# Strassen's method for the second layer's second product in two of three passes, on one Trainium2 core

## The chip, the cores and the metric

The kernel runs on one core of one Trainium2 chip. The metric is the device time of one execution in microseconds (us). Before the change the median of three runs was 808.29 us (807.82 to 812.54). Smaller is better.

## The reference, cut to what matters

An attention of Nyström type over four batches gives `x` of 2304 tokens by 512. Two layers without bias follow, each of two products:

```python
def _moe_ref(x, w_in, w_out):            # first layer, w_in 512 x 2048, w_out 2048 x 512
    h = x @ w_in
    sp = np.where(h > 20.0, h, np.log1p(np.exp(np.minimum(h, 20.0))))
    return ((h * np.tanh(sp)) @ w_out).astype(np.float32)

def _moe2_ref(x, w_in, w_out):           # second layer, the same shapes
    h = x @ w_in
    r = np.maximum(h, 0.0)
    g = r * r
    return (g @ w_out).astype(np.float32)
```

The change concerns the last line, `g @ w_out` of the second layer: 2304 x 2048 times 2048 x 512.

## The kernel before, in words

Both layers compute in float32 split in two: each operand is a high part (rounded to the matmul's fp32r type) and a low part (the rest), and a product is three matmuls, high by high, high by low and low by high. A matmul here loads 128x128 of one operand as weights and streams up to 512 columns of the other.

The second layer runs in three passes (index 0, 1, 2; called pass one, two and three below), each over 768 tokens as two blocks of 384. A pass goes over eight quads `Q{pass}{j}`, each 256 of the 2048 hidden columns. The first product of a quad already uses a form of Strassen's method with seven products (`Quad.p`, L995 to L1013): step `p(k)` is six matmuls of 384 columns into one PSUM room of the kind `y` (there are two, and a few of the first go elsewhere). ScalarE copies the first product (`s`, L1015), and VectorE makes the rest by seven additions `d(k)` of 128x384 (L1030), each of one product in PSUM to one sum in SBUF; a `d` frees the room that a later `p` needs. Then `r` squares the positive part (L1038, VectorE, 128x768, twice a quad), `h` makes the high part (L1043, ScalarE) and `g` the low part (L1048, VectorE).

The second product of a quad is `y(k)` for six blocks of 128 tokens (L1050 to L1063): the token block of `g` is the weight, and `w_out` streams, six matmuls of 512 columns each:

```python
for i in range(2):
    gh, gl, oh, ol = self.gh[:, i, ts], self.gl[:, i, ts], self.w[7 + 2 * i], self.w[8 + 2 * i]
    nc.tensor.matmul(ps, gh, oh, start=(j == 0 and i == 0), stop=False)
    nc.tensor.matmul(ps, gh, ol, start=False, stop=False)
    nc.tensor.matmul(ps, gl, oh, start=False, stop=(j == NQ - 1 and i == 1))
```

Over the eight quads the sums stay in PSUM, in three rooms of two banks (two of the kind `h`, one `at`). At the end of a pass `e(k)` (L1065) copies them to SBUF, and `o(k)` (L1072) sends them out.

The weights of the second layer are decoded from the inputs by `Unit` (steps `d, lo, st, ab, cl, ad, hi, lw`, L284 to L356), during the first layer and pass one. `hi` and `lw` make the high part on ScalarE and the low part on GpSimd; `sv` writes them to DRAM, and each quad of each pass loads seven tiles for the first product (`a`) and four for the second (`b`), 256 KB each, from there. `Forms` (`X{pass}`) makes the combinations of the inputs for the first product, with the low parts on GpSimd (`l`, L973).

The order of all steps of all engines is written out by hand in the string `PROGRAM`; no scheduler moves anything. Each engine runs its steps strictly in that order, and so does the one DMA queue, SyncE's.

Of the kernel before, what the change touches and what calls it, by code (L numbers as in the profile page):

```python
# [19 lines left out]
P = 128  # L20
TT = 384
# [13 lines left out]
NPASS = 3  # L35
MORE = 12
# [22 lines left out]
    d.cv U8.st f.tq@at B1.r0 c.ET B1.n1@y c.pv@y t0.c0 f.Tq e.sk B1.z1 B1.r1 U6.hi U5.cl U8.ab B1.n2@y e.tq@h B1.z2
    c.cr B1.r2 f.sq t0.c1 c.cv B1.n3@y+4 e.Tq d.mi U5.ad e.Sk B1.r3 U5.hi B1.z3 t0.g0 B1.n4@y+3 B1.r4 e.tl@y U6.lw  # L60
# [135 lines left out]
def nystrom_mish_relu2(  # L196
# [81 lines left out]
    class Unit:  # L278
# [876 lines left out]
```

## Time and profile before

| What | us |
|---|---|
| median of 3 runs | 808.29 (807.82 to 812.54) |
| the profiled execution, its own time | 807.35 |
| its span, first to last instruction | 805.5 |
| the first layer and the attention, up to the first product of pass one | 418.95 |
| pass one of the second layer | about 418.95 to 550 |
| passes two and three, to the last matmul | about 550 to 801 |

The times in the rows are microseconds from the start of the span. PE is TensorE's matmuls, PEld its weight loads, DVE is VectorE, ACT ScalarE, POOL GpSimd, SP SyncE. Matmuls are pipelined: one that is listed with 0.33 us starts its successor sooner, so what a matmul costs in a stream is the distance from one start to the next.

### The profile page before, as it was taken

The page shows a single profiled execution, that of the slowest core. Times are in us where ns is not written, and L with a number is a line of the kernel's source. Part 1 is how long each engine was busy: PE and PEld are TensorE (multiplying, and loading weights), DVE is VectorE, ACT ScalarE, POOL GpSimd, SP SyncE. Part 2 cuts the span into 40 slices and gives each one's busy share as a digit, 9 for nine tenths or more (in the row PEclk, how much of TensorE's full clock was granted, in tenths as well). Part 3 has the DMA queues.
Part 4 walks back from the last instruction along what each step waited for, and adds up shares of the span by engine and source line. Part 5 has one row for each costly group of instructions (what it writes and reads, how often), then busy time and mean ns, then how long its engine had stood idle before and what let it go on. Part 6 is the DMA issues. An engine that isn't in the chain of part 4 may idle for free.

```text
span 805.5 us, 14157 instructions
## 1 busy us (share of the span) xinstructions
PE 778.9 (97%) x5502; PEld 701.8 (87%) x5502; DVE 544.3 (68%) x898; ACT 338.3 (42%) x543; POOL 224.5 (28%) x172
## 2 busy tenths in 40 slices
PE   5798999999999999999998999999999999999997
PEld 4567988889999899999997899898889889798985
DVE  7989776756547967886978787767444454444552
ACT  5686898745443643647533423411122111211101
POOL 1345343231323643424462352531112000000000
PEclk9999999999999999999999999999999999999999
DMA  9972543222031455476568877879656666666603
GB/s 288 302 177 54 144 143 103 81 61 72 27 105 53 143 185 180 159 251 229 175 213 280 292 249 274 281 261 350 206 168 213 202 202 195 207 213 195 196 28 79
DMA packets 74435, 145.64 MB, mean 181 GB/s; under 512 B 8576, under 2 KB 21888, under 8 KB 74368
## 3 DMA queue, kind: packets, MB, share of 16 engines
q1 hardware_dynamic: 74368, 144.74, 56.3%
q8 instruction: 43, 0.70, 0.4%
q14 instruction: 24, 0.20, 0.1%
HBM read 116.92 MB, written 27.79 MB: 180 GB/s over the span
## 4 chain that ended last, share of the span: by engine, by line
PE 87%; DVE 6%; ACT 2%; DMA 2%; issue 1%; POOL 0%; DVEq 0%; ACTq 0%; POOLq 0%
PE y L793 8%; PE O L1061 8%; PE O L1060 8%; PE y L795 8%; PE y L794 8%; PE O L1059 8%; PE P L1007 7%; PE P L1008 7%; PE P L1009 7%; PE h L793 4%; PE h L795 4%; PE h L794 4%; PE m L778 2%; DMA rawwo<-in_moe_w_out_dram 1%; DVE lmq L434 1%
## 5 line engine op out<-in xcount | busy, mean ns | idle before, releaser
L1030 DVE TENSOR_TENSOR C<-U,P 128x384 f32<-128x384 f32 x96 | 51.8, 550 | 51.2 <-PE P L1009 50.0
L1043 ACT CAST gh<-C 128x768 fp32r<-128x768 f32 x48 | 39.3, 835 | 103.3 <-DVE C L1038 103.1
L1030 DVE TENSOR_TENSOR U<-U,P 128x384 f32<-128x384 f32 x72 | 39.8, 552 | 59.4 <-PE P L1009 58.4
L793 PE MATMUL h<-ah,mh 128*128 128x384 f32 (+1 forms) x256 | 79.1, 309 | 0.0
L795 PE MATMUL h<-ah,ml 128*128 128x384 f32 (+1 forms) x256 | 78.0, 305 | 0.0
L794 PE MATMUL h<-al,mh 128*128 128x384 f32 (+1 forms) x256 | 77.9, 304 | 0.0
L1048 DVE TENSOR_TENSOR gl<-C,gh 128x768 fp32r<-128x768 f32 x48 | 49.5, 1036 | 27.8 <-ACT gh L1043 27.4
L345 POOL TENSOR_TENSOR rawwo<-rawwo 128x512 int32<-128x512 int32 x32 | 37.0, 1158 | 109.7 <-DVE rawwo L329 68.5
L866 DVE TENSOR_TENSOR gl<-s,gh 128x768 fp32r<-128x768 f32 x48 | 53.6, 1117 | 20.1 <-ACT gh L856 20.0
L907 DVE TENSOR_TENSOR acc<-acc,y 128x384 f32<-128x384 f32 x72 | 39.1, 548 | 39.3 <-PE y L795 39.0
L1017 ACT COPY U<-P 128x384 f32<-128x384 f32 x24 | 11.5, 478 | 105.3 <-PE P L1009 105.3
L793 PEld LDWEIGHTS h<-ah,mh 128*128 128x128 f32 x256 | 48.5, 190 | 6.2 <-issue 2.7
L845 ACT ACTIVATE s<-h 128x768 f32<-128x768 f32 x48 | 38.8, 813 | 26.0 <-PE h L795 22.4
L795 PEld LDWEIGHTS h<-ah,ml 128*128 128x128 f32 x256 | 48.6, 190 | 0.0
L794 PEld LDWEIGHTS h<-al,mh 128*128 128x128 f32 x256 | 48.6, 190 | 0.0
L856 ACT CAST gh<-s 128x768 fp32r<-128x768 f32 x48 | 39.8, 834 | 15.8 <-PE y L795 15.4
L1038 DVE SCALAR_TENSOR_TENSOR C<-C 128x768 f32<-128x768 f32 x48 | 44.9, 958 | 0.8
L312 ACT ACTIVATE rawwo<-rawwo 128x512 f32<-128x512 uint32 x32 | 21.7, 678 | 30.2 <-DMA rawwo<-in_moe_w_out_dram 24.4
L342 POOL TENSOR_TENSOR wa<-rawwi 128x512 int32<-128x512 int32 x16 | 20.1, 1261 | 46.9 <-DVE rawwi L329 45.9
L315 DVE SCALAR_TENSOR_TENSOR rawwo<-rawwo 128x512 uint32<-128x512 uint32 x32 | 24.9, 778 | 10.5 <-ACT rawwo L312 10.3
L312 ACT ACTIVATE rawwi<-rawwi 128x512 f32<-128x512 uint32 x32 | 21.8, 684 | 21.3 <-DMA rawwi<-in_moe_w_in_dram 21.3
L335 POOL TENSOR_TENSOR wi<-rawwi 128x512 int32<-128x512 int32 x16 | 17.0, 1070 | 48.7 <-PE m L778 24.7
(653 smaller groups left out, 2415.6 us busy)
## 6 DMA issues: line engine op xcount, KB each, us to landing
rawwo<-in_moe_w_out_dram SPq DMA_DIRECT2D x32, 512.0 KB, 4.0
rawwi<-in_moe_w_in_dram SPq DMA_DIRECT2D x48, 256.0 KB, 4.2
v<-in_v_dram SPq DMA_DIRECT2D x16, 288.0 KB, 8.3
out_dram<-o SPq DMA_DIRECT2D x72, 64.0 KB, 2.5
rawwi<-in_moe_w_in_dram SPq DMA_DIRECT2D x8, 512.0 KB, 4.4
st<-wh SPq DMA_DIRECT2D x8, 512.0 KB, 3.3
st<-ws SPq DMA_DIRECT2D x8, 512.0 KB, 2.9
st<-wh SPq DMA_DIRECT2D x8, 384.0 KB, 3.7
```

The lines of the kernel that those rows point to most:

```text
L793: nc.tensor.matmul(ps, wh, rh, start=start, stop=False)
L794: nc.tensor.matmul(ps, wh, rl, start=False, stop=False)
L795: nc.tensor.matmul(ps, wl, rh, start=False, stop=stop)
L866: nc.vector.tensor_tensor(self.gl[:, sl, :], self.s[hf], self.gh[:, sl, :].bitcast(F32), ALU.subtract)
L1007: nc.tensor.matmul(ps[:, :TT], wh[:, c], xh[:, c, :], start=c == 0, stop=False)
L1008: nc.tensor.matmul(ps[:, :TT], wh[:, c], xl[:, c, :], start=False, stop=False)
L1009: nc.tensor.matmul(ps[:, :TT], wl[:, c], xh[:, c, :], start=False, stop=c == 1)
L1030: nc.vector.tensor_tensor(to, x, self.ps[i][:, :TT], ALU.add)
L1048: nc.vector.tensor_tensor(self.gl[:, k, :], flat(self.C[k]), self.gh[:, k, :].bitcast(F32), ALU.subtract)
L1059: nc.tensor.matmul(ps, gh, oh, start=(j == 0 and i == 0), stop=False)
L1060: nc.tensor.matmul(ps, gh, ol, start=False, stop=False)
L1061: nc.tensor.matmul(ps, gl, oh, start=False, stop=(j == NQ - 1 and i == 1))
```

## The change

Passes two and three group the quads in pairs, `Block` `Y{pass}{m}`: 768 tokens by 512 hidden columns by 512 outputs. Each of the three sides is halved, and the eight half products become seven (a form of Strassen's method with 7 products, 4 sums of each operand before and the rest after). All four pairs of pass two and the first three of pass three are done so; the last two quads of pass three and all of pass one keep the old form. A block's step `p(k)` is 18 matmuls of 256 columns (half of the 512 outputs) into one room of PSUM; a step `a(k)` adds the result to a sum in SBUF (or copies it, for the first block), and `Ending` (`Z1`, `Z2`) combines the seven sums to the outputs, on VectorE and GpSimd. The combinations of `g` are made by `t` (VectorE, both operands in SBUF, 128x768) after `r`; their high parts by `h` on ScalarE, their low parts by `l` on GpSimd (seven of each for a block). The old `g` stays for pass one and the last two quads.

`Second` (`K{j}`) makes the combinations of the weights on GpSimd during pass one (four `t` of 128x256 and two `l` of 128x512 for each of eight), ScalarE their high parts, and all seven forms go to DRAM (`seconds`). Passes two and three load 14 tiles of 256 KB a block from there. In pass one the decoded weights are used where they lie in SBUF, without the way through DRAM. `PROGRAM` is written anew as a whole.

```diff
         def sv(self):
-            x = pairs[self.f // 2]
+            q, c = divmod(self.f, 2)
+            d = seconds[q // 2]
             for i, t in enumerate(self.t):
-                nc.sync.dma_start(x.store[:, 7 + 2 * (self.f % 2) + i, :], t.bitcast(F32))
-            give(f"{self.nm}h", f"{self.nm}l")
+                t = t.bitcast(F32)
+                if c == 0:
+                    nc.sync.dma_start(d[:, 0, i, q % 2, :], t[:, :256])
+                else:
+                    nc.sync.dma_start(d[:, 1:3, i, q % 2, :], t.rearrange("p (f n) -> p f n", n=256))
...
+    seconds = [dram.tile([P, 7, 2, 2, 256], F32, tag=f"sc{m}", name=f"sc{m}") for m in range(NQ // 2)]
+    class Second:
...
+        def t(self, k):
...
+            x, y = [(b12, b11), (b22, T[0]), (b22, b12), (T[1], b21)][k]
+            nc.gpsimd.tensor_tensor(T[k], x, y, ALU.subtract)
+
+        def h(self, k):
+            self.high[k] = flat(page(f"sh{self.j}{k}", F32R))[:, :DM]
+            nc.scalar.copy(self.high[k], self.sums[k])
+
+        def l(self, k):
+            t = self.sums[k]
+            nc.gpsimd.tensor_tensor(t.bitcast(F32R), t, self.high[k].bitcast(F32), ALU.subtract)
...
+    class Block:
...
+        def r(self, k):
+            c = self.A[k]
+            nc.vector.scalar_tensor_tensor(c, c, 0.0, c, ALU.max, ALU.mult)
+            self.read(k)
+
+        def t(self, k):
+            to, x, y, op = ((4, 1, 3, ALU.add), (0, 4, 0, ALU.subtract), (1, 0, 1, ALU.subtract), (2, 2, 0, ALU.subtract))[k - 1]
+            nc.vector.tensor_tensor(self.room(to), self.A[x], self.A[y], op)
...
+        def h(self, k):
+            nc.scalar.copy(self.form(k)[0], self.A[self.src(k)])
...
+        def l(self, k):
+            hi, lo = self.form(k)
+            nc.gpsimd.tensor_tensor(lo, self.A[self.src(k)], hi.bitcast(F32), ALU.subtract)
...
+        def p(self, k, tag="h"):
+            f, w = ((0, 0), (1, 1), (6, 2), (2, 6), (3, 3), (4, 4), (5, 5))[k - 1]
+            t = big(f"O{self.n}{k}", tag)
+            self.ps[k] = flat(t)[:, :768].rearrange("p (c n) -> p c n", n=256)
+            (hi, lo), (wh, wl) = self.form(f), (self.W[w, i].rearrange("p (q n) -> p q n", n=256) for i in range(2))
+            for c in range(3):
+                ts = slice(c * P, (c + 1) * P)
+                for q in range(2):
+                    prod(self.ps[k][:, c, :], hi[:, q, ts], lo[:, q, ts], wh[:, q, :], wl[:, q, :], q == 0, q == 1)
...
+        def a(self, k):
+            p = self.turn
+            if self.m == 0:
...
+                nc.scalar.copy(total[p, k], self.ps[k])
+            else:
+                t = total[p, k]
+                nc.vector.tensor_tensor(t, t, self.ps[k], ALU.add)
+            give(f"O{self.n}{k}")
+
+    class Ending:
...
+        def u(self, k):
...
+            e = nc.gpsimd if k in (5, 7) else nc.vector
+            e.tensor_tensor(*S, op)
...
+        def e(self, k):
...
+            for d in range(2):
+                x, ds = total[self.p, ((2, 3), (4, 7))[h][d]], slice(d * 256, (d + 1) * 256)
+                nc.vector.tensor_tensor(self.t[h, c][:, ds], x[:, c, :], ps[:, ds], ALU.add)
...
         def y(self, k):
...
-                gh, gl, oh, ol = self.gh[:, i, ts], self.gl[:, i, ts], self.w[7 + 2 * i], self.w[8 + 2 * i]
-                nc.tensor.matmul(ps, gh, oh, start=(j == 0 and i == 0), stop=False)
+                gh, gl = self.gh[i][:, ts], self.gl[i][:, ts]
+                oh, ol = (self.w[7 + 2 * i], self.w[8 + 2 * i]) if p else pair[i].t
+                nc.tensor.matmul(ps, gh, oh, start=(first and i == 0), stop=False)
```

TensorE in pass two, before: behind step `p(2)` of quad 15 (`P152`) stands `y(3)` of quad 13 (`O11`, the room of token blocks 2 and 3), six matmuls of 512 columns.

```order
L1009 MATMUL P152_6827<-fh11_4761,q15w2_6650 128x384
L1059 MATMUL O11_6387<-q13w7_6595,gh13_6709 128x512
L1060 MATMUL O11_6387<-q13w8_6533,gh13_6709 128x512
L1061 MATMUL O11_6387<-q13w7_6595,gl13_6720 128x512
L1059 MATMUL O11_6387<-q13w9_6641,gh13_6709 128x512
L1060 MATMUL O11_6387<-q13w10_6696,gh13_6709 128x512
L1061 MATMUL O11_6387<-q13w9_6641,gl13_6720 128x512
L1059 MATMUL O12_6487<-q13w7_6595,gh13_6709 128x512
```

The same place now: behind `P152` stands the third product of the first block (`O103`; `b` are the block's weight forms, `ghr` and `glr` the high and low parts of a combination of `g`), 18 matmuls of 256 columns, of which the first three are shown.

```order
L1211 MATMUL P152_6906<-fh11_5011,q15w0_6782 128x384
L1212 MATMUL P152_6906<-fl11_6079,q15w0_6782 128x384
L1213 MATMUL P152_6906<-fh11_5011,q15w2_6714 128x384
L831 MATMUL O103_6918<-b1020_6799,ghr0_6486 128x256
L832 MATMUL O103_6918<-b1021_6668,ghr0_6486 128x256
L833 MATMUL O103_6918<-b1020_6799,glr0_6487 128x256
```

What moved: one product of the old form is finished in six long matmuls into a room that is kept for the whole pass; one of the new is 18 short ones into a room that VectorE or ScalarE has to empty.

GpSimd in pass one, before: the decoding of the weights of `w_out` (`rawwo`, `wo`) and low parts of the inputs' forms for pass two (`fl`).

```order
L345 TENSOR_TENSOR rawwo1_9_5380<-rawwo1_9_5380 128x512
L355 TENSOR_TENSOR wo1_9l_5529<-rawwo1_9_5380,wo1_9h_5528 128x512
L345 TENSOR_TENSOR rawwo1_8_5441<-rawwo1_8_5441 128x512
L973 TENSOR_TENSOR fl12_5567<-acc31_2733,fh12_4926 128x768
L355 TENSOR_TENSOR wo1_8l_5571<-rawwo1_8_5441,wo1_8h_5570 128x512
```

Now, for the same two units of weights (8 and 9), with the four combinations of `Second` for their pair (`sd40`, `sd41`) and the low part of an earlier one (`sd11`).

```order
L360 TENSOR_TENSOR wo1_8f_5564<-rawwo1_8_5424 128x512
L378 TENSOR_TENSOR wo1_6l_5534<-wo1_6f_5295,wo1_6h_5533 128x512
L1040 TENSOR_TENSOR sd40_5590<-wo1_8f_5564 128x256
L1040 TENSOR_TENSOR sd41_5610<-wo1_9f_5463,wo1_8f_5564 128x256
L1040 TENSOR_TENSOR sd40_5590<-wo1_9f_5463,sd40_5590 128x256
L1040 TENSOR_TENSOR sd41_5610<-sd40_5590,wo1_9f_5463 128x256
L1048 TENSOR_TENSOR sd11_4988<-sd11_4988,sh11_5326 128x512
L378 TENSOR_TENSOR wo1_9l_5637<-wo1_9f_5463,wo1_9h_5636 128x512
```

What moved: between the decoding of one unit and the next stand up to five more instructions of GpSimd, and the low part `wo1_9l`, which a step `y` of pass one reads, is behind them.

VectorE in pass three, before: the additions `d` (L1030) of quad 22, its two `r` (L1038), the first `g` (L1048).

```order
L1030 TENSOR_TENSOR C221_7594<-U22_7454,P224_7598 128x384
L1030 TENSOR_TENSOR C220_7555<-U22_7454,P223_7605 128x384
L1038 SCALAR_TENSOR_TENSOR C220_7555<-C220_7555 128x768
L1038 SCALAR_TENSOR_TENSOR C221_7594<-C221_7594 128x768
L1048 TENSOR_TENSOR gl22_7659<-C220_7555,gh22_7650 128x768
```

Now, around quads 23 and 24: additions `d` (L1241), a block's `r` (L1078) and `t` (L1083).

```order
L1078 SCALAR_TENSOR_TENSOR A212_7923<-A212_7923 128x768
L1083 TENSOR_TENSOR A200_7562<-A204_8013,A200_7562 128x768
L1078 SCALAR_TENSOR_TENSOR A210_7841<-A210_7841 128x768
L1241 TENSOR_TENSOR A211_7988<-U23_7990,P233_8084 128x384
L1078 SCALAR_TENSOR_TENSOR A213_7950<-A213_7950 128x768
L1241 TENSOR_TENSOR A220_8184<-U24_8128,P242_8174 128x384
L1241 TENSOR_TENSOR U24_8128<-U24_8128,P246_8165 128x384
```

What moved: between two `d`, on which TensorE's next products wait for room, stand up to three instructions of 128x768 whose operands all lie in SBUF, where before there was the pair of `r` and a `g`.

## Rows read from the trace of the kernel before

**Rows 1.** The page: each engine's busy time, share of the span and instructions.

```profile
PE 778.9 (97%) x5502; PEld 701.8 (87%) x5502; DVE 544.3 (68%) x898; ACT 338.3 (42%) x543; POOL 224.5 (28%) x172
```

**Rows 2.** Busy time by stretch: stretch, its length, busy us (instructions) PE, PEld, DVE, ACT, POOL; clock, DMA share, GB/s.

```profile
424.00:440.00 16.00, 13.72 (x72) 12.20 (x71) 14.02 (x25) 5.64 (x9) 5.25 (x4) 1.00 0.85 275
440.00:460.00 20.00, 19.93 (x100) 17.71 (x99) 17.02 (x26) 6.95 (x10) 5.65 (x5) 1.00 0.90 311
680.00:700.00 20.00, 18.42 (x91) 15.88 (x90) 10.41 (x16) 6.51 (x10) 0.00 (x0) 1.00 0.71 222
424.00:550.00 126.00, 123.66 (x620) 111.03 (x619) 98.34 (x151) 41.74 (x63) 50.58 (x34) 1.00 0.82 277
550.00:685.00 135.00, 134.93 (x671) 120.80 (x671) 67.96 (x101) 23.40 (x36) 11.42 (x7) 1.00 0.66 212
685.00:801.00 116.00, 113.63 (x556) 100.05 (x554) 53.65 (x79) 17.66 (x26) 0.00 (x0) 1.00 0.50 156
```

**Rows 3.** TensorE's matmuls in order of time (start, us): runs of 192, 384, 512 columns.

```profile
265.05 0.28 PE L795 MATMUL h<-ah,ml 128*128 128x192 f32 x1
...
266.06 0.27 PE L795 MATMUL h<-ah,ml 128*128 128x192 f32 x1
...
419.12 0.33 PE L1008 MATMUL P<-fl,q00w 128*128 128x384 f32 x1
...
424.32 0.33 PE L1008 MATMUL P<-fl,q00w 128*128 128x384 f32 x1
...
601.38 0.39 PE L1059 MATMUL O<-q12w,gh 128*128 128x512 f32 x1
...
603.92 0.39 PE L1061 MATMUL O<-q12w,gl 128*128 128x512 f32 x1
...
796.78 0.39 PE L1059 MATMUL O<-q27w,gh 128*128 128x512 f32 x1
...
800.64 0.39 PE L1061 MATMUL O<-q27w,gl 128*128 128x512 f32 x1
```

**Rows 4.** Groups by line and shape: count | busy us, mean ns | idle before, its releaser.

```profile
L1030 DVE TENSOR_TENSOR C<-U,P 128x384 f32<-128x384 f32 x96 | 51.8, 550 | 51.2 <-PE P L1009 50.0
L1038 DVE SCALAR_TENSOR_TENSOR C<-C 128x768 f32<-128x768 f32 x48 | 44.9, 958 | 0.8
...
L642 POOL TENSOR_TENSOR al<-At,ah 128x384 fp32r<-128x384 f32 x8 | 8.5, 1068 | 3.9 <-ACT ah L638 3.9
L642 POOL TENSOR_TENSOR al<-At,ah 128x192 fp32r<-128x192 f32 x8 | 4.8, 599 | 1.2 <-ACT ah L638 1.2
...
L355 POOL TENSOR_TENSOR wo_3l<-rawwo,wo_3h 128x512 fp32r<-128x512 f32 x2 | 2.6, 1296 | 2.0 <-ACT wo_3h L350 2.0
```

**Rows 5.** GpSimd and VectorE in order of time, at 404 and at 568 us.

```profile
404.46 1.84 POOL L973 TENSOR_TENSOR fl<-t,fh 128x768 fp32r<-128x768 f32 x1
404.48 0.56 DVE L907 TENSOR_TENSOR acc<-acc,y 128x384 f32<-128x384 f32 x1 [1.70 <-PE y L795]
404.95 2.17 DVE L866 TENSOR_TENSOR gl<-s,gh 128x768 fp32r<-128x768 f32 x1
406.27 3.11 POOL L934 TENSOR_TENSOR ws<-ws,wh 128x1024 fp32r<-128x1024 f32 x1
...
568.55 1.85 POOL L973 TENSOR_TENSOR fl<-t,fh 128x768 fp32r<-128x768 f32 x1 [18.39 <-ACT fh L968]
```

**Rows 6.** The chain of work that ended last, at the change from pass two to three, and its end.

```profile
684.00 0.70 DVE o L1068
...
685.32 1.28 ACT L1088
...
688.59 0.50 PE O L1061
...
801.06 0.58 ACT o L1068
```

**Rows 7.** A quad's loads of weights: issues, KB each, us to landing.

```profile
q15w<-st SPq DMA_DIRECT2D x11, 256.0 KB, 3.4
```

More of the change, by code (lines that the diff above doesn't have):

```diff
@@ L284, in __init__ @@
             self.by_rows = kind == "i" and li == 0
-            self.beside = False
+            self.beside, self.uses = False, 0
         def d(self, tag="raw"):
@@ L343, in ad @@
                 give(f"raw{self.nm}")
+            elif self.li:
+                self.whole = t = flat(page(f"{self.nm}f"))[:, :DM]
+                nc.gpsimd.tensor_tensor(t.bitcast(I32), up, low, ALU.add)
+                give(f"raw{self.nm}")
             else:
@@ L347, in hi @@
         def hi(self):
+            if self.li:
+                self.t = th, tl = [take("w", [DM], F32R, f"{self.nm}{t}") for t in "hl"]
+                nc.scalar.copy(th, self.whole)
+                return
             self.t = th, tl = [take("w", [DM], F32R, f"{self.nm}{t}") for t in "hl"]
@@ L982, in gone, with __init__, sv @@
             give(f"fh{self.p}{k}", f"fl{self.p}{k}")
+    seconds = [dram.tile([P, 7, 2, 2, 256], F32, tag=f"sc{m}", name=f"sc{m}") for m in range(NQ // 2)]
+    rest = dram.tile([P, 2, 4, DM], F32, tag="rest", name="rest")
+    class Second:
+        def __init__(self, j):
+            self.j, self.high = j, {}
+            self.sums = [None, None]
+        def t(self, k):
+            k -= 1
+            if k % 2 == 0:
+                self.sums[k // 2] = flat(page(f"sd{self.j}{k // 2}"))[:, :DM]
+            u0, u1 = (units[(NFG + self.j // 2) * 2 * FG + FG + self.j % 2 * 2 + i] for i in range(2))
+            b11, b12, b21, b22 = (u.whole[:, h * 256 : (h + 1) * 256] for u in (u0, u1) for h in range(2))
+            T = [s if s is None else s[:, h * 256 : (h + 1) * 256] for s in self.sums for h in range(2)]
+            x, y = [(b12, b11), (b22, T[0]), (b22, b12), (T[1], b21)][k]
[6 more added lines that the diff above has]
+            nc.gpsimd.tensor_tensor(t.bitcast(F32R), t, self.high[k].bitcast(F32), ALU.subtract)
+        def sv(self, k):
+            d = seconds[self.j // 2]
+            for i, t in enumerate((self.high[k].bitcast(F32), self.sums[k])):
+                nc.sync.dma_start(d[:, 3 + 2 * k : 5 + 2 * k, i, self.j % 2, :], t.rearrange("p (f n) -> p f n", n=256))
+            give(f"sd{self.j}{k}", f"sh{self.j}{k}")
@@ L1052, in y @@
             p, j = self.turn, self.j
-            if j == 0 and k % 2 == 0:
+            first = j == (NQ - 2 if p else 0)
+            if first and k % 2 == 0:
                 sums[p, k // 2] = big(f"O{p}{k // 2}", "at" if k == 4 else "h")
@@ L1112, in nystrom_mish_relu2 @@
     things |= {f"Q{p}{j}": Quad(p, j) for p in range(NPASS) for j in range(NQ)}
+    things |= {f"K{j}": Second(j) for j in range(NQ)}
+    blocks = {(p, m): Block(p, m) for p in (1, 2) for m in range(NQ // 2) if (p, m) != (2, NQ // 2 - 1)}
+    things |= {f"Y{p}{m}": x for (p, m), x in blocks.items()} | {f"Z{p}": Ending(p) for p in (1, 2)}
     things["x"] = Tables()
@@ L1122, in nystrom_mish_relu2 @@
             thing, _, step = step.partition(".")
-            number = [int(step[-1])] if step[-1].isdigit() else []
+            number = [int(step[len(step.rstrip("0123456789")) :])] if step[-1].isdigit() else []
             getattr(things[thing], step.rstrip("0123456789"))(*number, *([where] if where else []))
```

439 lines of the change are left out of this document (275 added, 164 removed).

## The prediction

> **What bounds the kernel now.** I read the page first: TensorE is busy 97% of the span, VectorE 68%, ScalarE 42%, GpSimd 28% [rows 1]. Since a busy TensorE need not be one at full rate, I then took the table of stretches. Pass one, with what is left of its start, is 126.00 us with TensorE busy 123.66, pass two 134.93 of 135.00, pass three 113.63 of 116.00 [rows 2]. So next to nothing is lost in waiting: in pass one at the start (13.72 of 16.00), and 1.58 us where pass three begins (18.42 of 20.00). The engines behind TensorE have room in passes two and three: VectorE 67.96 of 135.00 and 53.65 of 116.00, GpSimd 11.42 and nothing. In pass one they have less: VectorE 98.34 of 126.00, GpSimd 50.58. The granted clock is 1.00 throughout, the 2.4 GHz level. The kernel is bound by how fast TensorE starts its matmuls, and that is read from the order of time: nine steps from 265.05 to 266.06 make 0.112 us for one of 192 columns, thirty from 419.12 to 424.32 make 0.173 for 384, and for 512 columns eleven from 601.38 to 603.92 make 0.231, seventeen from 796.78 to 800.64 make 0.227 [rows 3]. I use 0.229 for 512.
>
> **The change part by part: TensorE's stream.** A pair of quads took 2 x 6 x 6 = 72 matmuls of 512 columns; a block takes 7 x 18 = 126 of 256. Seven blocks remove 504 and add 882. In columns that is one eighth less, but the shorter matmul must keep its price per column. Removed: 504 x 0.229 = 115.4 us. No row shows 256 columns. From 384 to 512 the distance grows by 0.054 to 0.058, so the line through them gives 0.116 to 0.120 for 256. But 192 columns stand at 0.112, above that line (it would give 0.09), so something else than columns sets the shortest distance, and 256 lies close to where it takes over. The other bound is the line from 192 to 384: 0.112 + (64 / 192) x 0.061 = 0.1326. I take 0.120, the upper end of the line from the two nearer in kind, since it still lies over the 0.112. Added: 882 x 0.120 = 105.8. Gain 9.6 us; with 0.116 it is 13.1, with 0.1326 a loss of 1.6. The break-even is 115.4 / 882 = 0.131.
>
> The Trainium skill (TensorE: Matmul & The Clock Gate, section LDWEIGHTS) states that a weight load takes its columns / 1.2 ns, 107 ns for 128, whatever streams. The 0.112 us of 192 columns agrees with such a floor [rows 3]. The same page (section Back-to-back issue gap) gives columns / 2.4 + 2.5 ns, an estimate of 109 ns for 256 and so a gain of 19 us instead of 9.6; but by it 384 columns would take 162 ns where the trace has 173, so the measured distances decide.
>
> **The change of pass.** Before, a pass ended by emptying the three rooms in which its sums lay. The chain shows it: two copies, a table load of 1.28 us and the next pass's first parts stand between 684.00 and TensorE's 688.59 [rows 6], and that stretch lost 1.58 us [rows 2]. Now each product of a block leaves PSUM at once, so there is no such point between passes two and three: 1.6 us less (at worst nothing).
>
> **VectorE.** In passes two and three it did seven `d` of 0.55 us, two `r` of 0.96 and two `g` of about the same a quad [rows 4]. Now a block costs 14 x 0.55 = 7.7 for `d`, four `r` 3.8, four `t` 3.8 (priced as `r`, 128x768 from SBUF), seven `a` 6.7 (twice the columns of a `d`: 0.55 + 0.40 = 0.95): 22.0 us. TensorE needs 14 x 6 x 0.173 = 14.5 and 126 x 0.120 = 15.1 for it, 29.6. For all of passes two and three: 112 `d` 61.6, 56 `r` and `t` 53.8, 35 `a` outside the first blocks 33, the last two quads' `r` and `g` 7.7, the four sums of the inputs' forms and the nine of `Ending` on VectorE 12.4, its pieces of 256 columns about 10 (24 at an estimated 0.42): 178 us in TensorE's 116.5 + 105.8 + 16.5 = 239. That fits, at 75% where there were some 50%.
>
> **GpSimd and the door it shares.** GpSimd gets seven `l` of 1.85 us a block [rows 5], with seven forms of pass three's inputs and four sums 60 x 1.85 = 111 us in the 239. In pass one it gets 32 combinations of 256 columns (0.60 for 192 and 1.07 for 384 give about 0.75) and 16 low parts of 512 (1.30) [rows 4]: 44.8 us on top of 50.6. That this is hidden rests on the spread: the first begin before pass one, the last end in pass two.
>
> It is not free beside VectorE. At 404.46 GpSimd starts a step of 1.84 us; a VectorE step with one operand in PSUM beside it takes its usual 0.56, but the one at 404.95 with both operands in SBUF takes 2.17 instead of about 0.96, ending 0.8 after GpSimd did, and the next of GpSimd, from 406.27, has to wait for that in turn [rows 5]. One of the two runs at a time. The kernel now adds just such steps on both sides, and behind a held VectorE step stand the `d` that free TensorE's two `y` rooms. Steps of this kind on VectorE in passes two and three: 56 `r` and `t`, 8 `r` and `g`, 13 sums, together 77. GpSimd runs 111 / 239 = 46% of the time, and a step that meets it waits half of 1.85 on average: 77 x 0.46 x 0.93 = 33 us of VectorE's waiting, which makes 211 of 239, 88%. How much of it reaches TensorE? Between nothing and 33 us. The nearest row is the stretch from 440 to 460 us, where VectorE is busy 17.02 of 20.00 beside GpSimd's 5.65, and TensorE loses 0.07 us [rows 2]: 0.35%, or 0.8 us in 239. I take twice that for the fuller door, 1.5 us.
>
> The Trainium skill (SBUF — State Buffer, section Who interferes with whom) calls this an exclusive lock: a VectorE instruction with two SBUF inputs and a GpSimd instruction that reads SBUF block each other fully. The 2.17 us agree with it. It speaks against this change, and it is the ground of the slower case below.
>
> **The rest.** The end: instead of a copy of 0.58 us [rows 6] two additions of 256 columns, an estimated 0.42 each, stand between the last matmul and the last transfer: 0.3 us more. Loads: 28 tiles a block instead of 22 for two quads, so the DMA engines' 0.66 and 0.50 [rows 2] become about 0.84 and 0.65; a tile lands in 3.4 us [rows 7], and the order issues it many steps ahead, so I cost them at nothing; without that cover each late tile costs up to those 3.4. ScalarE has room. The first layer stays as it is: nothing.
>
> **The sum.** 807.35 - 9.6 - 1.6 + 1.5 + 0.3 = 798.0 for the profiled execution, which lies 0.9 under the median of the runs: 798.9 us.
>
> **The rivals.** First, the short matmul is dear: if the floor and the columns add up rather than hide each other, 256 columns cost 0.1326, and the time is 798.9 + 882 x 0.0126 = 810.0. For it: 192 columns stand above the line. Against: 0.112 is still under 0.120.
>
> Second, slower: the shared door. The place is VectorE in passes two and three, the price up to 33 us. With all else as forecast, the gain without waits is 10.9, so from 11 of the 33 it is gone, and from 19 of them the kernel is slower by over 1%. At three quarters the time is 798.9 - 1.5 + 25 = 822.4. For it: 0.55 us of `d` against a `p` of 1.04 leave little when 2 to 3 us of held steps come between, and there are only two rooms. Against: the stretch at 440 us ran with VectorE at 85% and hardly a loss, and products of a block, 2.2 us each, stand between the `p`.
>
> Third, pass one is overfull: GpSimd's 95.4 us and 32 `r` and `g` of 0.96 alone fill the shared door for 126 us, as long as the pass, and a `y` now reads a low part that stands behind up to five added instructions. If in seven quads a quarter of the 4 x 0.75 + 2 x 1.30 = 5.6 us for one pair of units comes late, that is 9.8 us: 808.7.
>
> **How the numbers follow.** The forecast 0.58, its own range 793 to 803; the dear matmul 0.13; the shared door 0.13; the overfull pass one 0.16. Faster or slower by 1% is 8.1 us, about what a measurement of this kernel can tell from no change; the line lies at 800.2, inside the forecast's own range. Faster: 0.45 of the forecast's 0.58 and 0.02 of smaller losses in pass one, 0.47. Slower: the shared door, 0.13. Same: the rest, 0.40. The range goes from 791 (0.116 for the short matmul, and no new waits) to 811, over the dear matmul and the overfull pass, and leaves most of the shared door out.
>
> **What would show it.** Right: matmuls of 256 columns 0.120 us apart; TensorE over 99% busy in passes two and three and none of the 1.6 us at their border; `r` and `t` often over 0.96 us while TensorE goes on. Wrong: a distance of 0.13; gaps before `P` released by VectorE's `d` behind a long `r` or `t`; in pass one gaps before `O` released by GpSimd.

## The result, and the profile after

The changed kernel takes 819.99 us (median of 4 runs, 818.22 to 822.03) beside 809.11 (807.82 to 812.54) for the kernel before: a ratio of 1.0129, interval 1.0087 to 1.0170. It is slower by 1.3%, where the interval leaves 0.9 to 1.7%. The forecast was 798.9, range 791 to 811, so both the number and the sign were wrong.

The profiled execution takes 819.18 us with a span of 817.4. Its engines, beside [rows 1]:

```profile
PE 771.3 (94%) x5880; PEld 714.2 (87%) x5880; DVE 602.4 (74%) x957; ACT 369.9 (45%) x588; POOL 394.1 (48%) x273
```

TensorE works 7.6 us less and yet the span is 11.9 longer. Where that lies is read from the stretches; the columns are those of [rows 2].

```profile
420.00:550.00 130.00, 127.93 (x648) 115.38 (x648) 101.28 (x146) 45.12 (x72) 88.13 (x65) 1.00 0.85 272
550.00:660.00 110.00, 109.98 (x739) 107.48 (x738) 83.46 (x106) 37.85 (x54) 78.96 (x44) 1.00 0.83 277
660.00:774.00 114.00, 113.31 (x799) 111.96 (x799) 89.68 (x120) 30.60 (x42) 56.49 (x29) 1.00 0.73 233
774.00:794.00 20.00, 18.22 (x72) 14.26 (x71) 8.67 (x11) 3.80 (x5) 2.62 (x1) 0.91 0.20 50
794.00:817.00 23.00, 0.03 (x1) 0.00 (x0) 3.40 (x10) 0.00 (x0) 0.00 (x0) 0.58 0.19 68
```

From 550 to 774 us TensorE loses almost nothing: it is busy 109.98 of 110.00 and 113.31 of 114.00, with VectorE at 76 to 79% and GpSimd at 72 and 50%. Then come 20 us with a lower clock, and 23 us in which TensorE does nothing. The short matmuls, in order of time (start first), to be held against [rows 3]:

```profile
599.83 0.28 PE L832 MATMUL O<-b,ghr 128*128 128x256 f32 x1
...
601.03 0.28 PE L833 MATMUL O<-b,glr 128*128 128x256 f32 x1
```

Between these two lie ten steps in 1.20 us: 0.120 for 256 columns. The new groups of VectorE and GpSimd, in the form of [rows 4] (busy, mean ns):

```profile
L1106 POOL TENSOR_TENSOR glr<-A,ghr 128x768 fp32r<-128x768 f32 x49 | 98.3, 2025 | 66.8 <-ACT ghr L1101 52.7 <-PE P L1213 6.3 <-DVE A L1241 4.5
...
L1083 DVE TENSOR_TENSOR A<-A,A 128x768 f32<-128x768 f32 x28 | 36.7, 1311 | 0.2
L1078 DVE SCALAR_TENSOR_TENSOR A<-A 128x768 f32<-128x768 f32 x28 | 33.2, 1194 | 0.1
...
L1132 DVE TENSOR_TENSOR sum<-sum,O 128x768 f32<-128x768 f32 x32 | 30.0, 949 | 10.7 <-PE O L833 10.7
```

The chain of work that ended last, from 771 us on, answers to [rows 6]:

```profile
771.54 5.12 DMA q26w<-rest
776.71 0.53 PE O L1279
...
793.81 0.24 PE O L1280
794.41 0.41 DVE o L1178
794.82 0.33 DVEq L1374
795.15 2.32 DVE o L1178 x7
```

First, a load of a weight tile of quad 26 (5.12 us) is late. TensorE's starts, and a stretch behind them:

```profile
774.53 0.40 PE L1278 MATMUL O<-q26w,gh 128*128 128x512 f32 x1
776.71 0.53 PE L1279 MATMUL O<-q26w,gh 128*128 128x512 f32 x1 [1.78 <-DMA q26w<-rest]
...
780.45 0.40 PE L1279 MATMUL O<-q26w,gh 128*128 128x512 f32 x1
```

```profile
777.00:780.00 3.00, 3.00 (x8) 2.33 (x8) 2.93 (x4) 1.56 (x3) 0.76 (x1) 0.51 0.67 170
```

TensorE loses 1.95 us (774.53 to 776.71 between two starts, where 0.23 is usual). The next nine matmuls take 3.74 us from start to start, eight of them 0.43 us each, where nine usually take 2.07: 1.7 us more. The granted clock there is 0.51, the 1.2 GHz level. Then, at the end, VectorE adds the outputs and SyncE sends them. VectorE and SyncE's queue in order of time:

```profile
788.63 0.75 DVE L1178 TENSOR_TENSOR o<-sum,O 128x256 f32<-128x256 f32 x2 [4.91 <-PE O L1280]
794.07 3.40 DVE L1178 TENSOR_TENSOR o<-sum,O 128x256 f32<-128x256 f32 x10 [4.68 <-PE O L1280]
```

```profile
794.85 10.65 SPq L1185 DMA_DIRECT2D out_dram<-o  x7
```

In the kernel before, the copies of the outputs (there, what the additions are here) stood each behind the last `y` of its own block, and 24 pieces of 64 KB went out from 789.78 on:

```profile
789.78 13.61 SPq L1076 DMA_DIRECT2D out_dram<-o  x24
```

Here `PROGRAM` has all six additions behind the last `y`. VectorE makes the first at 788.63, as its block's products are done by then, and the other five behind the last matmul. The first block's transfer stands in SyncE's queue behind that of a later block, so all 7 transfers, 256 KB for a whole block, start at 794.85 or after. The span ends at 817.4. The stretches of that time:

```profile
798.00:802.00 4.00, 0.00 (x0) 0.00 (x0) 0.00 (x0) 0.00 (x0) 0.00 (x0) 0.50 0.25 93
802.00:806.00 4.00, 0.00 (x0) 0.00 (x0) 0.00 (x0) 0.00 (x0) 0.00 (x0) 0.50 0.26 102
806.00:810.00 4.00, 0.00 (x0) 0.00 (x0) 0.00 (x0) 0.00 (x0) 0.00 (x0) 0.50 0.26 100
810.00:816.00 6.00, 0.00 (x0) 0.00 (x0) 0.00 (x0) 0.00 (x0) 0.00 (x0) 0.50 0.14 56
```

A DMA share of 0.25 is 4 of the 16 engines, 0.14 about 2. In the trace's records of completions the seven transfers end 2.56 us apart, from 801.12 to 816.50: they go one behind the other on the same few engines while the rest are idle. A transfer of 256 KB goes to 4 x 32 rows of DRAM, its outermost dimension 4; the one block that crosses a batch goes out in two halves of 2 x 32 rows.

The difference of the two spans adds up from starts of matmuls. The first and the last of this stretch, after:

```profile
420.34 0.33 PE L1211 MATMUL P<-fh,q00w 128*128 128x384 f32 x1
...
793.64 0.39 PE L1280 MATMUL O<-q27w,gl 128*128 128x512 f32 x1
```

First form product of pass one: 418.95 before, 420.34 after (+1.4). From there to the last matmul: 381.69 and 373.31 (-8.4). From the last matmul to the end: 4.86 and 23.76 (+18.9). Together +11.9, the whole of it. The matmuls gave what they were to give; the end took back about twice as much.

### The profile page after: what moved, and what is told of

Same layout as the page of the kernel before. It is cut to its first block, busy times and chain, and to the rows that moved or that the text cites. A ratio compares the mean times of both kernels' runs of the same rounds, so it can differ in the third digit from the quotient of the medians.

```text
span 817.4 us, 15299 instructions
## 1 busy us (share of the span) xinstructions
PE 771.3 (94%) x5880; PEld 714.2 (87%) x5880; DVE 602.4 (74%) x957; ACT 369.9 (45%) x588; POOL 394.1 (48%) x273
## 4 chain that ended last, share of the span: by engine, by line
PE 85%; DMA 6%; DVE 4%; issue 1%; ACT 1%; POOL 0%; SPq 0%; DVEq 0%; POOLq 0%; ACTq 0%
PE y L831 8%; PE y L832 8%; PE y L833 8%; PE P L1211 7%; PE P L1213 7%; PE P L1212 7%; PE h L831 4%; PE h L833 4%; PE h L832 4%; PE O L831 4%; PE O L833 4%; PE O L832 4%; DMA rawwi<-in_moe_w_in_dram 4%; PE O L1280 3%; PE O L1279 3%; PE O L1278 3%
## 5 line engine op out<-in xcount | busy, mean ns | idle before, releaser
L1106 POOL TENSOR_TENSOR glr<-A,ghr 128x768 fp32r<-128x768 f32 x49 | 98.3, 2025 | 66.8 <-ACT ghr L1101 52.7
L831 PE MATMUL O<-b,ghr 128*128 128x256 f32 x294 | 83.2, 283 | 0.0
L833 PE MATMUL O<-b,glr 128*128 128x256 f32 x294 | 83.0, 282 | 0.0
L832 PE MATMUL O<-b,ghr 128*128 128x256 f32 x294 | 83.0, 282 | 0.0
L1101 ACT CAST ghr<-A 128x768 fp32r<-128x768 f32 x49 | 40.4, 837 | 79.9 <-DVE A L1083 33.5
L904 DVE TENSOR_TENSOR gl<-s,gh 128x768 fp32r<-128x768 f32 x48 | 51.3, 1071 | 20.6 <-ACT gh L894 20.6
L1241 DVE TENSOR_TENSOR U<-U,P 128x384 f32<-128x384 f32 x72 | 39.7, 551 | 31.9 <-PE P L1213 28.4
L831 PEld LDWEIGHTS O<-b,ghr 128*128 128x128 f32 x294 | 56.0, 190 | 0.6 <-ACT o L1289 0.3
L833 PEld LDWEIGHTS O<-b,glr 128*128 128x128 f32 x294 | 56.1, 191 | 0.0
L832 PEld LDWEIGHTS O<-b,ghr 128*128 128x128 f32 x294 | 56.0, 191 | 0.0
L1241 DVE TENSOR_TENSOR A<-U,P 128x384 f32<-128x384 f32 x56 | 30.2, 549 | 23.6 <-PE P L1213 19.4
L894 ACT CAST gh<-s 128x768 fp32r<-128x768 f32 x48 | 40.0, 835 | 15.9 <-PE y L833 15.7
```

Source lines behind the costliest of these rows:

```text
L831: nc.tensor.matmul(ps, wh, rh, start=start, stop=False)
L832: nc.tensor.matmul(ps, wh, rl, start=False, stop=False)
L833: nc.tensor.matmul(ps, wl, rh, start=False, stop=stop)
L894: nc.scalar.copy(gh, s)
L904: nc.vector.tensor_tensor(self.gl[:, sl, :], self.s[hf], self.gh[:, sl, :].bitcast(F32), ALU.subtract)
L1101: nc.scalar.copy(self.form(k)[0], self.A[self.src(k)])
```

## The experiments

Theory: the change as such is right, and two things in how outputs leave take its gain: the transfers' shape (4 engines of 16) and the order at the end. Rivals are named with each. The time "outputs" in the table runs from the first issue of pass three's outputs to the end of the span, "stream" from the first form product of pass one to the last matmul, "tail" from there to the end, all of the profiled execution. Each ratio is to runs of the kernel before on the same chip in the same series (medians 808.82 to 809.95); it is taken over all runs and is not the quotient of the two medians. Spans are given to 0.1 us, so a tail is good to about 0.05.

| Kernel | median, us | ratio to before, interval | stream | tail | outputs |
|---|---|---|---|---|---|
| before | 809.11 | 1 | 381.69 | 4.86 | 15.7 |
| after | 819.99 | 1.0129, 1.0087 to 1.0170 | 373.31 | 23.76 | 22.6 |
| sums early | 811.46 | 1.0014, 0.9991 to 1.0038 | 374.19 | 12.97 | 22.4 |
| small pieces | 806.61 | 0.9966, 0.9937 to 0.9994 | 368.33 | 14.67 | 13.5 |
| both | 802.02 | 0.9903, 0.9868 to 0.9938 | 371.09 | 5.30 | 13.4 |
| rows in order | 800.61, one run | none | 368.31 | 7.86 | 6.7 |
| pass two small | 815.34 | 1.0084, 1.0052 to 1.0115 | 368.39 | 24.06 | 22.9 |
| before, merged | 816.47 | 1.0095, 1.0059 to 1.0131 | 382.51 | 12.36 | 23.2 |
| order, small | 798.41 | 0.9865, 0.9827 to 0.9903 | 368.51 | 5.37 | 13.5 |
| order, two queues | 796.18 | 0.9836, 0.9809 to 0.9864 | 368.58 | 4.60 | 12.7 |
| whole sums | 798.34 | 0.9869, 0.9847 to 0.9891 | 370.03 | 4.64 | 12.7 |
| sum on VectorE | 797.28 | 0.9884, 0.9838 to 0.9929 | 368.53 | 4.66 | 12.7 |
| before, two queues | 810.00 | 1.0004, 0.9984 to 1.0024 | 382.71 | 4.35 | 15.2 |

**Sums early** (`e1_sums_early`). Only the order of the end: each addition right behind the `y` that fills its half of a PSUM room (two blocks share one).

```diff
-    ... Q27.g0 Q27.y4 Q27.y2 Z2.u2 Z2.u3 Q27.y0 Z2.u7 Z2.u4 Q07.o0 Q26.y3 Z2.u8 Q27.y3
-    Q26.y1 Q27.y1 Q26.y5 Q27.y5 x.m Z2.u6 Z2.e2 Z2.e4 Z2.o4 Z2.o2 Z2.e0 Z2.o0 Z2.e3 Z2.o3 Z2.e1 Z2.o1 Z2.e5 Z2.o5
+    ... Q27.g0 Q07.o0 Z2.u2 Z2.u3 Z2.u7 Z2.u4 Z2.u8 x.m Z2.u6 Q27.y2 Z2.e2 Z2.o2 Q27.y0 Z2.e0 Z2.o0 Q27.y4 Z2.e4 Z2.o4
+    Q26.y3 Q27.y3 Z2.e3 Z2.o3 Q26.y1 Q27.y1 Z2.e1 Z2.o1 Q26.y5 Q27.y5 Z2.e5 Z2.o5
```

> Only the end of PROGRAM is written in another order: in pass three each final addition and its transfer stand right behind the last matmul into its half of a PSUM room, before the first matmul into the other half. Theory (order): in the changed kernel the first of these additions starts at 788.6 and the other five wait for the last matmul at 794; with the new order they run between about 784 and 795, and the transfers of 1.57 MB, which ran at about 100 GB/s, start near 785 instead of 795, so the span falls from 817.4 by 8 to 11 us, to 806 to 809. Rival (the transfers alone): whatever the order, the last of the six 256 KB transfers takes 10 us after the last matmul, so at most 3 us are gained.

Measured: 811.46, the span 810.5, a little over what was expected.

```profile
788.11 11.18 SPq L1186 DMA_DIRECT2D out_dram<-o  x7
```

The first output is issued at 788.11 in place of 794.85, 6.7 us sooner, and the span is 6.9 us shorter; the seven transfers take 22.4 us, as long as in the changed kernel (22.6). So the order matters only as the start of a fixed price. This execution's first form product starts at 423.34, 3.0 us later than in the changed kernel; counted from there the end comes 9.9 us sooner, inside the 8 to 11 that were expected.

**Small pieces** (`e2_small_outs`). Only the shape: outputs of passes two and three in four pieces of 32 rows.

```diff
-            for b in sorted({b for b, _ in idx}):
-                ms = [m for m in range(P // LM) if idx[m][0] == b]
+            for ms in [[m] for m in range(P // LM)]:
+                b = idx[ms[0]][0]
                 nc.sync.dma_start(
                     out[b * S : (b + 1) * S, :].rearrange("(l i) d -> i l d", i=SEG)[idx[ms[0]][1] : idx[ms[-1]][1] + 1],
                     self.t[h, c][ms[0] * LM : (ms[-1] + 1) * LM, :],
                 )
```

> Only the outputs of passes two and three leave in pieces of 64 KB (32 rows of 2 KB), as before the change, where the changed kernel sends up to 256 KB at once. Theory (shape): a transfer of 4 x 32 rows uses few of the 16 engines, so 1.57 MB take some 16 to 20 us whatever is in flight; in pieces of 64 KB the queue's issue of about 0.57 us each sets the pace, 24 x 0.57 = 13.7 us from 794.9, end near 811, and the loads between 750 and 776 are no longer held by such transfers, so the stretch in which TensorE waits for the last weights (1.95 us at 774.5 and nine matmuls at half clock) goes too, 2 to 4 us more: span 807 to 811. Rival (rate): 100 GB/s is what transfers out get in any shape; span stays at 816 to 818.

Measured: 806.61, the span 805.7, a little under what was expected. The outputs take 13.5 us instead of 22.6, and the stream falls to 368.3: the late load of quad 26, its stall and the slow matmuls are gone. The end of its SyncE queue and the stretch beside it:

```profile
792.24 11.15 SPq L1185 DMA_DIRECT2D out_dram<-o  x24
```

```profile
793.00:803.00 10.00, 0.00 (x0) 0.00 (x0) 1.86 (x6) 0.00 (x0) 0.00 (x0) 0.64 0.54 139
```

The share is 0.54 rather than 0.25. SyncE's issues now take 11.15 of the 13.5 us, 0.46 for each of 24.

**Both** edits in one kernel (`e3_both`):

> Both edits: early final additions and pieces of 64 KB. If the tail is order and shape together, the last transfer is issued within 3 us of the last matmul as before the change (4.9 us from last matmul start to the end of the span), and TensorE's stream ends at 790 to 794: span 795 to 799, faster than the kernel before by 6 to 10 us. If something else holds the end, the span stays above 803.

Measured: 802.02, faster than before; the span of the profiled execution, 797.5, is as expected. The tail is 5.3 us, but TensorE stands for 2.62 us at 781.2, ahead of `Q26.y3`: the additions of the first blocks stand behind sums that they don't need.

**Rows in order** (`e4_rows_in_order`). A transfer of 256 KB goes to 128 consecutive rows, so the rows of the output stand in other places than they should; the run is a measurement of the transfers alone.

```diff
-            for b in sorted({b for b, _ in idx}):
...
+            r0 = 2 * p * TT + k * P
+            for a, e in ((0, 64), (64, P)) if any(x != idx[0][0] for x, _ in idx) else ((0, P),):
+                nc.sync.dma_start(out[r0 + a : r0 + e, :], self.t[h, c][a:e, :])
```

> The changed kernel, with the outputs of passes two and three written as 128 consecutive rows of the output instead of 4 x 32 rows that lie 18 apart: same sizes, same order, other places in DRAM (the output's rows stand elsewhere than the reference's). Theory (shape): with one run of 128 rows all 16 engines share a transfer; the seven transfers end 3 to 4 us after their issue, span 800 to 805 instead of 817.4. Rival (size of 256 KB, or rate of writes): the span stays at 815 to 818.

Measured: 800.61, the span 798.8, in spite of the late additions. Its end:

```profile
792.15 3.77 SPq L1185 DMA_DIRECT2D out_dram<-o  x7
```

```profile
794.00:798.00 4.00, 0.00 (x0) 0.00 (x0) 0.77 (x3) 0.00 (x0) 0.00 (x0) 0.66 0.86 300
```

The same seven transfers of the same bytes in rows of the same 2 KB, share 0.86 at 300 GB/s in place of 0.26 at 100. The size of a transfer and the number of issues are not the cause; the way the rows are laid out is. What differs in the instruction is the outermost dimension, 128 or 64 in place of 4 or 2, and that the rows are neighbours. "Small pieces" tells the two apart: its rows lie 18 apart as in the changed kernel, its outermost dimension is 32, and its share of 0.54 is more than 4 engines can make. The trace's records of single rows agree: up to 16 are in flight at once there, in the changed kernel's end mostly 4 and never over 6. So rows need not be neighbours.

The Trainium skill (DMA: Bandwidth & Descriptors, section Why a DMA increments its semaphore by 16 and not by 1) says that a transfer runs on the largest number of engines, up to 16, that divides the outermost dimension of both sides. The shares agree: 0.25 and 0.26 for an outermost 4, 0.14 for 2. One transfer with the 32 rows outermost would need the tile's partitions in another order; that was not tried.

**Pass two small** (`e5_pass_two_small`). As "small pieces", but for pass two's outputs alone (`if p == 1`).

> The changed kernel with only pass two's outputs in pieces of 64 KB; pass three's outputs stay in transfers of 256 KB. Theory (the wide transfers cost in two places: those of pass two hold back the loads of pair 26's weights and so TensorE, those of pass three stretch the end): from the first form product of pass two to the last matmul 368 to 369 us, as where all are small (changed kernel: 373.3), no load of pair 26 on the chain of waits, no matmuls at the lower clock near 777; but from the last matmul to the end 23 to 24 us as in the changed kernel. Span 812 to 816 and time 814 to 817. Rival (all of the loss sits in the end, the late load is an accident of other traffic): the stream stays at 373 us and the span at 817.

Measured: 815.34, as expected. The stream falls to 368.39, as in "small pieces", and the tail stays at 24.06. So pass two's wide transfers, issued from 705 to 774 us, were what made quad 26's load late (they took about 4.9 us of the stream), and pass three's lie in the tail. How they did it stands in the waits of the changed kernel's SyncE queue, where L1226 issues the last loads of quads 26 and 27, and in its issue of the late load beside that of "pass two small":

```profile
SPq L1226 <- DMA out_dram<-o: 8.7, 3, 4.2
```

```profile
771.54 0.34 SPq L1226 DMA_DIRECT2D q26w<-rest  x1
```

```profile
769.17 0.38 SPq L1228 DMA_DIRECT2D q26w<-rest  x1
```

Three times, 8.7 us together and 4.2 us at the longest, the queue stood at such a load until an output had landed (0.2 us in "pass two small"). Counted from the first form product (420.34 and 421.15) the late load is issued 3.2 us later than in "pass two small". By the trace's records of completions it lands 5.0 us later. So for the larger part it was late because it was issued late, and only for the rest because its own transfer was slow.

**Before, merged** (`e7_before_merged`). The kernel before, its outputs of passes two and three in the changed kernel's shape.

```diff
-            for m in range(P // LM):
-                b, i = divmod((2 * p * TT + k * P) // LM + m, SEG)
+            idx = [divmod((2 * p * TT + k * P) // LM + m, SEG) for m in range(P // LM)]
+            for ms in [[m for m in range(P // LM) if idx[m][0] == b] for b in sorted({b for b, _ in idx})] if p else [
+                [m] for m in range(P // LM)
+            ]:
+                b = idx[ms[0]][0]
                 nc.sync.dma_start(
-                    out[b * S : (b + 1) * S, :].rearrange("(l i) d -> i l d", i=SEG)[i],
-                    outs[p, k][m * LM : (m + 1) * LM, :],
+                    out[b * S : (b + 1) * S, :].rearrange("(l i) d -> i l d", i=SEG)[idx[ms[0]][1] : idx[ms[-1]][1] + 1],
+                    outs[p, k][ms[0] * LM : (ms[-1] + 1) * LM, :],
```

> The kernel before with one edit: outputs of passes two and three issued as the changed kernel does it, 4 x 32 rows in one transfer of 256 KB (7 issues in pass three in place of 24). Theory (a transfer whose outer dimension is 4 runs on 4 engines at 84 ns a row, 5 us and more for 256 KB, and two that overlap share them): the last transfer starts some 2 us behind the last matmul and needs at least 5 us more, with the one ahead of it still on the same engines: 8 to 13 us from last matmul to end in place of 4.9; span 808 to 814, time 811 to 817. Rival (fewer issues help here, where SyncE's 24 issues take 13.6 us): span 802 to 805.

Measured: 816.47, the ratio 1.0095, as expected. The merged outputs alone, without the new method in the second product, cost 0.6 to 1.3% (some 7 us; the tail grows from 4.86 to 12.36). Its queue and a stretch of its end:

```profile
790.33 12.39 SPq L1079 DMA_DIRECT2D out_dram<-o  x7
```

```profile
803.00:812.00 9.00, 0.00 (x0) 0.00 (x0) 0.00 (x0) 0.00 (x0) 0.00 (x0) 0.68 0.21 75
```

**The order mended** (`e6_order_two_queues`, `e8_order_small`). Additions behind only the sums that they need, with small pieces; in the first of the two every second piece of pass three goes out from ScalarE's queue, in the second all from SyncE's. In these two kernels the block of step `Z2.e4` is added ahead of the two sums that belong to it (`Z2.u7`, `Z2.u8`), so that block's output comes from unfinished sums and is not what the reference gives.

```diff
+    ... Q07.o0 Z2.u2 Z2.u3 Z2.u4 x.m Z2.u6 Q27.y2 Z2.e2 Z2.o2 Q27.y0 Z2.e0 Z2.o0 Q27.y4 Z2.e4 Z2.o4 Z2.u7 Z2.u8
...
-                nc.sync.dma_start(
+                (nc.scalar if p == 2 and ms[0] % 2 else nc.sync).dma_start(
```

> The changed kernel with all outputs of passes two and three in pieces of 64 KB, the additions of the output's first half drawn up behind their own products and behind only those four sums that they need (the two sums of the other half follow), and every second piece of pass three issued from ScalarE's queue. Theory: the stall of 2.6 us ahead of the second half's products, in which the first half's additions waited for a GpSimd sum that they do not need, shrinks to under 0.6; the stream is 369 us; SyncE's queue of 24 issues at 0.46 us no longer sets the end; 4 us from last matmul to end. Span 793 to 796, time 795 to 799. Rival (ScalarE's issues are dearer, or the engines of the transfers are the limit): same as with one queue.

> As e6_order_two_queues, but all issues from SyncE's queue. Theory: stall ahead of the second half's products under 0.6 us in place of 2.6, so the last matmul comes 2 us sooner after the first form product (369 us in place of 371.1); the queue of 24 issues starts 2 us sooner and sets the end. Span 794.5 to 797, time 797 to 800. Rival (the stall comes from the room of the sums in PSUM and not from the waiting sums): stall and stream stay at 2.6 and 371 us, span 797.5.

Measured: 796.18 and 798.41, both as expected. The stall ahead of `Q26.y3` is under 0.1 us in both, so it came from the sums that stood ahead of the additions and not from the room; with the second queue the tail is 4.60 us in place of 5.37.

**Whole sums** (`e9_whole_sums`). The order put right: `Z2.u7` behind `Z2.u3`, `Z2.u8` ahead of `Q27.y4` and `Z2.e4`.

> As e6_order_two_queues, with the order put right: the two sums of the other half stand ahead of the addition of the fourth block, which needs them (in e6_order_two_queues and e8_order_small that block was added from unfinished sums). Theory: the room that the fourth block's addition holds is only wanted by the last six products, so its later place costs nothing: span 793 to 795.5, time 795 to 798, ratio to before 0.982 to 0.987. Rival (the shortcut carried the gain): the stall ahead of the second half's products comes back with 2 us and more, span 796 to 798.

Measured: 798.34, the span 796.5. That is the rival's span: the stall is back, with 1.57 us where the rival had 2 and more. The stalled matmul, VectorE's four sums ahead of the additions, and the lines of the sums (min, median and max in ns) show why:

```profile
783.80 0.50 PE L1279 MATMUL O<-q26w,gh 128*128 128x512 f32 x1 [1.41 <-DVE o L1179]
```

```profile
777.64 5.45 DVE L1153 TENSOR_TENSOR sum<-sum,sum 128x768 f32<-128x768 f32 x4
```

```profile
L1153 DVE TENSOR_TENSOR sum<-sum,sum x5: 945/958/2477, 777.6 to 784.3; 128x768 f32<-128x768 f32 x5
L1153 POOL TENSOR_TENSOR sum<-sum,sum x1: 2607/2607/2607, 779.7 to 779.7; 128x768 f32<-128x768 f32 x1
```

`u7` runs on GpSimd, 2.61 us from 779.66, and one of VectorE's sums beside it takes 2.48 us, in place of 0.95. It is the shared door of the prediction.

**Sum on VectorE** (`e11_sum_on_vector`). Pass three's `u7` on VectorE instead, behind the first additions (shown against "whole sums").

```diff
-    Z2.u7 Z2.u4 x.m Z2.u6 Q27.y2 Z2.e2 Z2.o2 Q27.y0 Z2.e0 Z2.o0 Z2.u8 Q27.y4 Z2.e4 Z2.o4
+    Z2.u4 x.m Z2.u6 Q27.y2 Z2.e2 Z2.o2 Q27.y0 Z2.e0 Z2.o0 Z2.u7 Z2.u8 Q27.y4 Z2.e4 Z2.o4
...
-            e = nc.gpsimd if k in (5, 7) else nc.vector
+            e = nc.gpsimd if k == 5 or (k == 7 and self.p == 1) else nc.vector
```

> As e9_whole_sums, with the other half's first sum in pass three on VectorE in place of GpSimd, drawn up behind the additions of the first half (two blocks of it). Theory (shared door: in e9_whole_sums the GpSimd sum of 2.61 us at 779.66 held a VectorE sum to 2.48 us in place of 0.95, and the second half's products waited 1.57 us for what stood behind it): without the GpSimd step no sum of VectorE takes over 1.0 us, the stall is under 0.2 us, the stream from first form product to last matmul 368.5 us in place of 370.0; span 793 to 795.5, time 795 to 797.5. Rival (the stall is VectorE's own row of sums, whatever GpSimd does): stall over 1 us, span 796 to 798.

Measured: 797.28, the span 795.5, the stream 368.53:

```profile
778.13 3.93 DVE L1153 TENSOR_TENSOR sum<-sum,sum 128x768 f32<-128x768 f32 x4
```

```profile
L1153 DVE TENSOR_TENSOR sum<-sum,sum x6: 951/958/959, 778.1 to 784.3; 128x768 f32<-128x768 f32 x6
```

The same four sums take 3.93 us in place of 5.45; no sum is held and the stall is under 0.1 us. The edit changes both the engine of `u7` and its place, and either alone would take the GpSimd step from beside the held sum; which of the two is needed was not tried. In the medians the step is too small to see (0.9884, interval 0.9838 to 0.9929, beside 0.9869); it is shown by the trace alone. This kernel and "whole sums" are 1.2 and 1.3% faster than the kernel before the change (intervals 0.7 to 1.6% and 1.1 to 1.5%).

**Before, two queues** (`e10_before_two_queues`). Every second piece of pass three from ScalarE's queue, in the kernel before.

> The kernel before with one edit: every second piece of pass three's outputs issued from ScalarE's queue. Theory (the gain of e9_whole_sums over before is the change's shorter stream; the second queue alone brings under 2 us): last matmul where it was, 3 to 4.5 us from it to the end in place of 4.9; span 803.5 to 805.5, time 806 to 809.5. Rival (the second queue is what beats before): span under 800.

Measured: 810.00, ratio 1.0004. The span, 808.8, lies over what was expected, though the tail is 0.5 us shorter: the first form product of this execution starts at 421.75 rather than 418.95. The second queue is not what beats before.

## Why the prediction was wrong, and where it was right

**The matmuls: right.** The forecast was 0.120 us for 256 columns; 845 distances between two short matmuls in the trace have a mean of 0.1198. The dear short matmul (0.1326) and a cheaper one (0.116) did not come. By the prediction's own sum this is 9.6 us. The formula that the prediction quotes for this distance (Trainium skill, TensorE: Matmul & The Clock Gate, section Back-to-back issue gap) is given there for a matmul by itself, which is not this case.

**The stream.** The forecast for the stream was a gain of 9.6 for the matmuls and 1.6 for the change of pass, less 1.5 for waits: 9.7. With the shape and the order of the outputs put right it gains 13.2 us (368.53 in "sum on VectorE" beside 381.69). The stall where pass three began (1.49 us at 685.9) went, as was said, and waits of over 0.05 us sum up to 5.00 us in place of 7.21: 2.2 less, where 1.6 less and 1.5 more were forecast. So the forecast was too small here, and it was the waits that it had too high.

**The shared door in passes two and three: the mechanism right, the size too large.** `r` takes 1194 ns and `t` 1311 ns beside the 958 of [rows 4]. With 0.95 us as the time of a step that is not held, the 28 `r` and 28 `t` of the blocks wait 16.9 us, the last two quads' `r` 3.3 (two of 2.6) and the sums 0.5: 20.7 us where 33 were forecast. To TensorE next to nothing came: it loses 0.7 us in 550 to 774, and of that VectorE's part is 0.3. Its waits there (us in all, times, the longest):

```profile
PE P L1211 <- DMA q27w<-st: 0.4, 1, 0.4
PE P L1211 <- DVE U L1241: 0.3, 1, 0.3
```

The slower rival by this door did not happen. The measured slowdown has the sign that this rival was to have, but by another cause. The door did act at two narrow places: at 400.59, where a `g` of the first layer took 3.08 us beside a GpSimd step and TensorE lost 1.56, and in the end's sums. The first of these:

```profile
400.48 2.38 POOL L972 TENSOR_TENSOR ws<-ws,wh 128x1024 fp32r<-128x1024 f32 x1
400.59 3.08 DVE L904 TENSOR_TENSOR gl<-s,gh 128x768 fp32r<-128x768 f32 x1
```

**Pass one overfull: no.** GpSimd's work in 420 to 550 rose from 51.13 to 88.13 us, and TensorE lost 2.07 of 130.00, where it had lost 2.34 before.

**The end: the step that failed.** The prediction says: "The end: instead of a copy of 0.58 us [rows 6] two additions of 256 columns, an estimated 0.42 each, stand between the last matmul and the last transfer: 0.3 us more." The additions do take 0.42. But the step counted what stands behind the last matmul as if the rest of the end were unchanged, and it was not: the five other blocks' additions and all transfers were moved behind the last products, and the transfers were cast in a shape that runs on 4 engines, or 2. The measured term is +18.9 us. Small pieces without the new order leave 14.67 of tail, the new order without small pieces 12.97, both together 5.30.

**The loads: a second part of the same omission.** "I cost them at nothing; without that cover each late tile costs up to those 3.4." One tile was late by much, and one (of quad 27) by 0.4 us. What the prediction left out is that loads share their queue with the outputs: SyncE stood 8.7 us at loads until outputs had landed. The late tile of quad 26 cost TensorE 1.95 us, and 1.7 more in nine matmuls at the lower clock; with pass two's outputs in small pieces the stream is 4.9 us shorter.

Put into the sum, the measured terms make it come out, as they must, since they are parts of the same two spans: 798.0 and 18.6 more for the end (18.9 in place of 0.3) is 816.6; the stream's 8.4 in place of 9.7 gives 817.9; the 1.4 us later first product (the held `g` at 400.59 cost 1.56, and starts vary by more than that) 819.3, where the profiled execution took 819.18. That "sum on VectorE", with its end mended, lies near the forecast (797.28 beside 798.9) is in part luck: its stream gains 3.5 us more than was forecast, and its first form product starts 3.4 us later than before.

## What to carry to other kernels

Read an edit's transfers like its arithmetic: how many instructions, how many bytes, and what the outermost dimension is on either side. Fewer and larger transfers can be the slower ones. Where one stands at the end of a kernel its whole duration is on the path, and anywhere else it can hold up the queue in which loads stand. And count a kernel's end as a schedule of its own: what is first allowed to leave, on which queue, and in which order the sums that it needs are made.

## What the runs showed that was not expected

An output of 256 KB in rows of 2 KB went out at 100 GB/s where the rows were grouped 4 x 32, and at 300 GB/s where they followed each other. The kernel before becomes 0.95% slower by that shape alone.

After the stall of 1.95 us at 774.5 eight matmuls of TensorE stood 0.43 us apart, where 0.23 is usual, and the granted clock from 777 to 780 was 0.51, the 1.2 GHz level. In "both" a stall of 2.62 us at 781.2 was not followed by such matmuls; the granted clock from 784 to 787 was 1.00. What tells the two apart was not tried and stays open.

The start varies: the first form product of pass one starts at 418.63 to 423.34 us in the profiled executions, at 418.95 and 421.75 in two kernels whose first 400 us are the same (before, and "before, two queues"). Single spans that lie closer than that tell nothing; the distances within one trace do.
